# Attention and a SoLU feed-forward on one core: two spreads rescheduled, one PSUM bank exchanged, the last results stored in quarters

## The chip, the core and the metric

The kernel runs on one core of a Trainium2 chip. The metric is the device time of one execution in microseconds (us); a kernel's time is the median of its runs. Five engines run side by side, each in its own order: TensorE (PE, matrix products), VectorE (DVE), ScalarE (ACT), GpSimd (POOL) and SyncE (SP), which here issues nearly all transfers. TensorE writes into PSUM[...].

## The reference

```python
q_n, k_n = rmsnorm(q, g_q), rmsnorm(k, g_k)          # 8 x 12 heads, 448 x 64
scores = scale * np.matmul(q_n, k_n.transpose(0, 1, 3, 2))
attn = softmax(scores)
x = np.matmul(attn, v)           # bridged to 3584 tokens x 768
h = x @ w_in                     # 3584 x 1024
solu = h * softmax(h)
ln = (solu - mu) / np.sqrt(var + 1e-06) * g_ln
return ln @ w_out                # 3584 x 768
```

The names `softmax` and `rmsnorm` stand for the reference's own lines, which subtract the row's maximum and divide by the root of the mean square. All arithmetic is float32 in the kernel.

## The kernel before

`fast_path` does the work in three stages that follow each other on TensorE.

**Stage one**, to about 331 us, is attention. It leaves x in DRAM (`xd`).

**Stage two**, 331.7 to about 584 us, is `x @ w_in` and the SoLU with its normalisation. The 3584 tokens are 28 tiles t of 128 rows, two to a group g, so 14 groups; tiles 24 and 25 are group 12, tiles 26 and 27 group 13. A group is multiplied as a 2 x 2 block product with seven products instead of eight (`products`, p1 to p7, six matmuls of 512 columns each). They accumulate in four banks called A, B, C and D. `mul` (L974) takes banks A and C from the tag "t" (three tiles of two banks each, of which one bank is used) and B and D from the tag "o" (two tiles of one bank). B is used by two products: p5 starts it, `plus` (L998, VectorE) reads it, and p3, the last product of a group, writes on into the same bank. `plus` keeps a running row maximum, and p4 and p3 end with `done(1)` and `done(0)`, which complete the rows of tiles 2g+1 and 2g.

Each finished tile then goes through steps on other engines: `ff_max` (VectorE, at once), `ff_exp` (ScalarE, L1053), `ff_mult` (VectorE, L1057), `ff_moments` (VectorE L1065 to L1070, then two small GpSimd instructions, L1071 a power and L1073 the shift), `ff_norm` (ScalarE, L1077) and `ff_spread` (L1084). A spread is one VectorE transpose of 128 x 1024 (L1086) into a buffer `ub`, and four stores of 128 KB from it to DRAM (`ud`, L1089) on SP.

**Stage three**, from about 585 us, is the product with `w_out`. Four tiles make one n, so seven of them; for each n, `load_u` (L1128) brings eight pieces of 256 KB back from `ud`, `make` (L1144) turns them into operands called a11, a12, a22, s1 to s4 (a11, a12 and a22 are ScalarE copies, L1149, L1151 and L1153; the others VectorE), and `outer_product` (L1177) runs seven block products P1 to P7 of seven small products each (four matmuls of 192 columns). Its banks are A to C under tags of their own, placed over the eight banks that stage two gives back; in the kernel before, the first A of stage three is the bank that B of group 13 held. `plus` of this stage (L1202) moves a bank out: as a ScalarE copy (L1206; the temporaries q1, u2 and u3) for the first products, else as a VectorE sum (L1208). p7's result u3 must be out of bank A before p4 of the same product may write on into it. Finished quarters of an output block are summed on VectorE (L1226, L1238, L1246, L1208), and `store_y` (L1258) stores a block of 256 x 384 in one transfer of 384 KB. Of the seven products P2, P3 and P4 end a block; a fourth block, C22, is summed by `both` (L1264).

**The order of the work** is written out by hand. `unit(f)` emits one piece and moves a counter `now` by four; in stage three each slot moves it by one. `later(u, f)` puts f behind the piece that ends u units later. The pieces emitted this way are each engine's order, and no engine overtakes within it. `done` schedules the five steps of a tile by the list WAITS (L1117): 1, 2, 3, 5 and 7 units later. With seven units the spread of tile 25 comes after the last but one product of stage two, those of tiles 24, 27 and 26 fall into stage three, after its slots 3, 19 and 23. SP's order at the seam is: the four stores of tile 25; six loads for n = 0 (tiles 2 and 3 in two halves, then the second halves of tiles 0 and 1, which are a12); the four stores of tile 24; six loads for n = 1; the stores of tile 27; two loads; the stores of tile 26. The two a12 copies are placed at slots 10 and 11.

Of the kernel before, what the change touches and what calls it, by code (L numbers as in the profile page):

```python
# [366 lines left out]
def fast_path(  # L367
# [24 lines left out]
    nc = tc.nc  # L392
    B, H, S, D = q.shape
    DM, DFF = moe_w_in.shape
    P = 128
# [6 lines left out]
    HO = DM // 2  # L402
    NT = B * S // P
    NG = NT // 2
# [563 lines left out]
    def products(g, done):  # L968


        k = {}
        n = DFF // 2

        def mul(bank, a, i, begin=True):  # L974
            a11, a12, a21, a22 = gs[g, "A"]
            sm = gs[g, "s"]
            a = {"a11": a11, "a12": a12, "s3": a21, "a22": a22, "s1": sm[:, 0], "s2": sm[:, 1], "s4": sm[:, 2]}[a]
            if begin:
                tag = "t" if bank in "AC" else "o"
                k[bank] = ps_t.tile([P, 512], FP32, tag=tag, name=bank, bufs=3 if tag == "t" else 2)[:, 0:n]  # L980
            for c in range(HD):
                nc.tensor.matmul(  # L982
                    k[bank], a[:, c], w_in[i][:, c],
                    start=begin and c == 0, stop=c == HD - 1, skip_group_check=not begin,
                )

        def part(name, bank):
            k[name] = sums_in.tile([P, 512], FP32, tag="part", name=name, bufs=4)[:, 0:n]
            nc.scalar.copy(k[name], k[bank])

        def plus(row, col, bank, x):
            t = 2 * g + row
            d = mt.setdefault(t, {})
            out = half_of(t, col)
            top = small.tile([P, 1], FP32, tag="top", name="top")
            nc.vector.tensor_tensor_reduce(  # L998
                out, k[bank], k[x], 1.0, d.get("top", -3.4e38), OP.add, OP.max, top
            )  # L1000
            d["top"] = top

        def p1():
            mul("A", "a11", 0)
            part("q1", "A")

        def p2():
            mul("C", "a12", 1)
            plus(0, 0, "C", "q1")

        def p6():
            mul("A", "s2", 5, False)
            part("u2", "A")

        def p5():
            mul("B", "s1", 3)

        def p7():
            mul("A", "s3", 4, False)
            part("u3", "A")  # L1020
            plus(1, 1, "B", "u3")

        def p4():
            mul("D", "a22", 6)
            plus(1, 0, "D", "u3")
            done(1)

        def p3():
            mul("B", "s4", 2, False)
            plus(0, 1, "B", "u2")  # L1030
            done(0)

        return {1: p1, 2: p2, 3: p3, 4: p4, 5: p5, 6: p6, 7: p7}

    def half_of(t, i):
        d = mt.setdefault(t, {})
        if "h" not in d:
            d["h"] = big.tile([P, DFF], FP32, tag="h", name="h", bufs=3)
        return d["h"][:, i * DFF // 2 : (i + 1) * DFF // 2]
# [4 lines left out]
    def ff_max(t):  # L1044
        d = mt[t]
        d["nmax"] = small.tile([P, 1], FP32, tag="hmax", name="hmax")
        nc.vector.tensor_scalar(d["nmax"], d["top"], -1.0, None, OP.mult)  # L1047
# [46 lines left out]
    def in_parts():  # L1094
        def done(g, i):
            t = 2 * g + i
            ff_max(t)
            for x, f in zip(WAITS, (ff_exp, ff_mult, ff_moments, ff_norm, ff_spread)):
                later(x, lambda f=f: f(t))

        p = [products(g, lambda i, g=g: done(g, i)) for g in range(NG)]
        parts = [p[0][1], p[0][2]]
        for g in range(NG):
            turn = [p[g][6], p[g][5], p[g][7], p[g][4], p[g][3]]
            x = len(parts)
            if g + 1 < NG:
                turn[3:] = [p[g + 1][1], p[g][4], p[g + 1][2], p[g][3]]
            parts += turn
            if g + 1 < NG:
                follow(parts, x, lambda g=g: sizes(g + 1))  # L1110
                follow(parts, x + 1, lambda g=g: block_sums(g + 1, 0))
                follow(parts, x + 2, lambda g=g: block_sums(g + 1, 1))
            if g + 2 < NG:
                follow(parts, x + 4, lambda g=g: load_x(g + 2))
        return parts

    WAITS = (1, 2, 3, 5, 7)  # L1117
    ORDER = ("P1", "P5", "P6", "P2", "P7", "P3", "P4")
    STEP = 7
    PLACES = (0, 4, 8, 10, 12, 16, 20)  # L1120
    NS = NT // 4
    KC = HF // 2
    N2 = HO // 2
    HALVES = {"P1": ("a11", 0), "P2": ("a12", 1), "P6": ("s2", 5), "P5": ("s1", 3), "P7": ("s3", 4), "P3": ("s4", 2), "P4": ("a22", 6)}
    last = {}
    us = {}
# [50 lines left out]
    def outer_product(n, name, q):  # L1177


        operand_name, area = HALVES[name]  # L1180
        k = {}

        def mul(bank, a, i, begin):
            x = us[n, operand_name]
            sm = us.get((n, operand_name, "sums"))
            a = {
                "a11": x[:, 0, 0:KC], "a12": x[:, 0, KC:], "a22": x[:, 1, KC:],
                "s1": sm and sm[:, 0], "s2": sm and sm[:, 1], "s3": sm and sm[:, 2], "s4": sm and sm[:, 3],
            }[a]
            if begin:  # L1190
                tag = f"{bank}{q % 2}" + (str(q // 2 % 2) if bank == "A" else "")
                k[bank] = last["ps"].tile([P, 512], FP32, tag=tag, name=bank)[:, 0:N2]
            for c in range(KC):
                nc.tensor.matmul(  # L1194
                    k[bank], a[:, c].rearrange("p a i -> p (a i)"), w_out[:, area, i, c],
                    start=begin and c == 0, stop=c == KC - 1, skip_group_check=not begin,
                )

        def quarter(x, t, i):
            return x[:, t, i * N2 : (i + 1) * N2]  # L1200

        def plus(out, bank, t, i):  # L1202

            x = {"P6": "Q1", "P2": "Q1", "P7": "U2", "P4": "U3", "P3": "V"}.get(name)
            if x is None:
                nc.scalar.copy(out, k[bank])  # L1206
            else:
                nc.vector.tensor_tensor(out, k[bank], quarter(us[n, x], t, i), OP.add)  # L1208

        def temp(x):  # L1210
            k[x] = last["u"].tile([P, N2], FP32, tag=x, name=x, bufs=3)
            return k[x]

        def result(t, i):
            return quarter(us[n, name], t, i)

        def p1():
            mul("A", "a11", 0, True)
            plus(temp("q1"), "A", 0, 0)

        def p2():
            mul("C", "a12", 1, True)
            us[n, name] = out_tile(name)
            if name in ("P1", "P6", "P7"):
                us[n, {"P1": "Q1", "P6": "U2", "P7": "U3"}[name]] = us[n, name]
            nc.vector.tensor_tensor(result(0, 0), k["C"], k["q1"], OP.add)  # L1226

        def p6():
            mul("A", "s2", 5, False)
            plus(temp("u2"), "A", 0, 1)  # L1230

        def p5():
            mul("B", "s1", 3, True)

        def p7():
            mul("A", "s3", 4, False)
            plus(temp("u3"), "A", 1, 1)
            nc.vector.tensor_tensor(result(1, 1), k["B"], k["u3"], OP.add)  # L1238

        def p4():  # L1240
            mul("A", "a22", 6, False)
            plus(result(1, 0), "A", 1, 0)

        def p3():
            mul("B", "s4", 2, False)
            nc.vector.tensor_tensor(result(0, 1), k["B"], k["u2"], OP.add)  # L1246
            if name in ("P2", "P3", "P4"):
                store_y(n, us[n, name], *{"P2": (0, 0), "P3": (0, 1), "P4": (1, 0)}[name])

        return [p1, p2, p6, p5, p7, p4, p3]  # L1250

    def out_tile(name):
        tag = "huhuhubb"[len(turns) % 8]
        turns.append(tag)
        x = big.tile([P, DFF], FP32, tag=tag, name=name, bufs=2 if tag == "b" else 3)
        return x[:, 0 : 2 * HO].rearrange("p (t n) -> p t n", t=2)

    def store_y(n, x, k, i):  # L1258
        r = (4 * n + 2 * k) * P
        nc.sync.dma_start(  # L1260
            out[r : r + 2 * P, i * HO : (i + 1) * HO].rearrange("(t p) n -> p t n", p=P), x
        )

    def both(n, x, t):  # L1264

        if (n, x) not in us:
            us[n, x] = out_tile(x)
        nc.vector.tensor_tensor(us[n, x][:, t], us[n, "U2" if x == "V" else "U3"][:, t], us[n, "P5"][:, t], OP.add)
        if x == "C22" and t == 0:
            store_y(n, us[n, x], 1, 1)  # L1270

    def follow(p, i, f):
        g = p[i]

        def both():
            g()
            later(1, f)

        p[i] = both
# [7 lines left out]
    def later(units, f):  # L1287
        todo.append((now + 4 * units, f))
# [49 lines left out]
    with tc.manual_schedule():  # L1338
# [233 lines left out]
        for n in range(NS):  # L1572
            base = period * n
            for i, name in enumerate(ORDER):
# [4 lines left out]
                x = HALVES[name][0]  # L1579
# [118 lines left out]
```

## Time and profile before

| | |
|---|---|
| median of three runs | 825.22 us |
| the runs | 825.22, 827.1, 821.57 us |
| the profiled execution | 824.41 us, of which its span 822.2 |
| TensorE's clock in it | 0.997 of full speed |
| stage two on TensorE | 331.7 to 584.4 us of the span |
| stage three on TensorE | 585.2 to 816.0 us of the span |
| last store of a result | issued at 816.43 us, landed 3.9 us later |

Times within a profile are microseconds from the start of its span. A row of the timeline is: start, duration, engine, source line, operation, output tile <- input tiles, shapes, how many instructions are merged; in brackets how long the engine stood idle before, and what released it. A row of the waits is: engine, tile and line that waited <- what ended the wait: microseconds in total, times, longest. The engine name SPq is SP's queue of transfers. "Landing" is the time from the issue of a transfer to its completion.

### The profile page before, as it was taken

Reading aid. Unit: us, or ns where it says so; the run is one execution under the profiler, and the core shown is the slowest. Engines: PE = TensorE matmul, PEld = TensorE weight load, DVE = VectorE, ACT = ScalarE, POOL = GpSimd, SP = SyncE. Lnnn points to the kernel's source line nnn. Section 1 sums busy time; section 2 is a strip of 40 time slices with the busy share of each in tenths; the row PEclk is TensorE's granted clock in tenths of the full one; section 3 lists DMA queues with packets and bytes.
Section 4 is the critical chain, followed back from the end, with each engine's and each line's share of the span. In section 5 each row is a group of like instructions: output and inputs, shape, how many; then the busy total and the mean of one; then the engine's idle time right before and its main releaser. Section 6 shows DMA issues by size and latency. Waiting matters only on the chain.

```text
span 822.2 us, 14988 instructions
## 1 busy us (share of the span) xinstructions
PE 800.5 (97%) x5030; PEld 468.7 (57%) x5030; DVE 618.1 (75%) x1217; ACT 474.6 (58%) x785; POOL 468.7 (57%) x635
## 2 busy tenths in 40 slices
PE   8989999999999999999999999999799999999996
PEld 4333444433334443444444444444499999999996
DVE  6867888887788888377878766677886866866945
ACT  6667778776777767366667644444424464464420
POOL 1334545555555647333356467777387777877861
PEclk9999999999999999999999999999999999999999
DMA  7678777777777663335665335552448466376312
GB/s 132 142 134 200 145 183 177 176 153 171 154 176 180 126 156 117 89 102 125 189 169 150 91 98 133 136 140 70 140 142 269 130 207 231 128 241 200 128 59 82
DMA packets 271938, 122.74 MB, mean 149 GB/s; under 512 B 190444, under 2 KB 257004, under 8 KB 271852
## 3 DMA queue, kind: packets, MB, share of 16 engines
q1 hardware_dynamic: 256668, 111.79, 52.9%
q10 hardware_dynamic: 15184, 9.90, 4.5%
q8 instruction: 42, 0.69, 0.4%
q14 instruction: 44, 0.36, 0.1%
HBM read 84.94 MB, written 36.70 MB: 148 GB/s over the span
## 4 chain that ended last, share of the span: by engine, by line
PE 84%; SPq 2%; DVE 2%; issue 2%; POOL 1%; DMA 1%; ACT 1%; POOLq 0%; ACTq 0%; DVEq 0%
PE A L1194 15%; PE A L982 13%; PE o L865 10%; PE s L812 10%; PE B L982 8%; PE B L1194 8%; PE D L982 4%; PE C L982 4%; PE sm L884 4%; PE C L1194 4%; SPq L634 2%; PE s L825 2%; PE o L854 2%; POOL ss L674 1%; DMA ur<-ud 1%
## 5 line engine op out<-in xcount | busy, mean ns | idle before, releaser
L802 ACT ACTIVATE E<-s 128x896 f32<-128x896 f32 x168 | 139.0, 935 | 14.9 <-PE s L812 14.6
L812 PE MATMUL s<-qkT 64*64 64x448 f32 x1152 | 121.3, 548 | 1.5 <-ACT E L802 0.9
L865 PE MATMUL o<-E,v 128*64 128x448 f32 x576 | 113.5, 543 | 0.0
L674 POOL COPY ss<-part 32x56 f32<-32x56 f32 x88 | 42.1, 478 | 97.9 <-DVE part L664 95.2
L713 POOL TENSOR_TENSOR qkn<-qk,ny 128x896 f32<-128x896 f32 x46 | 77.1, 1697 | 28.2 <-DMA qk<-in_k_dram 12.0
L1071 POOL TENSOR_TENSOR he<-he,mhalf 128x1 f32<-128x1 f32 x28 | 28.1, 1005 | 106.7 <-DVE he L1070 106.2
L812 PEld LDWEIGHTS s<-qkT 64*64 64x64 f32 x1152 | 47.5, 163 | 61.1 <-ACT E L802 31.3
L865 PEld LDWEIGHTS o<-E,v 128*64 128x64 f32 x576 | 39.2, 137 | 72.7 <-issue 66.4
L1194 PE MATMUL B<-w_out,sums 128*128 128x192 f32 x392 | 80.5, 328 | 0.0
L1194 PE MATMUL A<-w_out,sums 128*128 128x192 f32 x392 | 80.0, 327 | 0.4 <-DVE u L1208 0.4
L982 PE MATMUL B<-w_in,xsum 128*128 128x512 f32 x168 | 76.7, 592 | 0.0
L982 PE MATMUL A<-w_in,xg 128*128 128x512 f32 x168 | 74.7, 593 | 0.0
L1053 ACT ACTIVATE u<-h,hmax 128x1024 f32<-128x1024 f32 x28 | 32.2, 1148 | 65.2 <-DVE hmax L1047 65.2
L1194 PEld LDWEIGHTS B<-w_out,sums 128*128 128x128 f32 x392 | 67.0, 191 | 0.1
L1194 PEld LDWEIGHTS A<-w_out,sums 128*128 128x128 f32 x392 | 66.2, 190 | 0.9 <-POOL sums L1175 0.6
L664 DVE TENSOR_REDUCE part<-sq 128x28 f32<-128x896 f32 x46 | 48.7, 1080 | 8.8 <-ACT sq L656 6.7
L982 PEld LDWEIGHTS B<-w_in,xsum 128*128 128x128 f32 x168 | 31.9, 190 | 40.2 <-issue 38.3
L982 PEld LDWEIGHTS A<-w_in,xg 128*128 128x128 f32 x168 | 31.8, 190 | 40.2 <-issue 39.1
L723 DVE STREAM_TRANSPOSE qkT<-qkn 128x896 f32<-128x896 f32 x46 | 48.9, 1093 | 6.6 <-POOL qkn L713 6.6
L839 DVE TENSOR_TENSOR es<-E 128x896 f32<-128x896 f32 x48 | 53.3, 1112 | 0.5 <-ACT E L802 0.5
L656 ACT ACTIVATE sq<-qk 128x896 f32<-128x896 f32 x46 | 43.6, 985 | 8.7 <-DMA qk<-in_k_dram 6.7
L1194 PE MATMUL A<-w_out,s 128*128 128x192 f32 x224 | 45.6, 326 | 0.0
(151 smaller groups left out, 1625.3 us busy)
## 6 DMA issues: line engine op xcount, KB each, us to landing
ur<-ud SPq DMA_DIRECT2D x60, 256.0 KB, 4.7
ud<-ub SPq DMA_DIRECT2D x112, 128.0 KB, 2.3
xd<-xo SPq DMA_DIRECT2D x24, 448.0 KB, 3.7
qk<-in_q_dram SPq DMA_DIRECT2D x184, 56.0 KB, 2.5
qk<-in_k_dram SPq DMA_DIRECT2D x184, 56.0 KB, 2.4
v<-in_v_dram SPq DMA_DIRECT2D x24, 384.0 KB, 4.4
out_dram<-P SPq DMA_DIRECT2D x21, 384.0 KB, 3.8
raw<-in_moe_w_in_dram SPq DMA_DIRECT2D x12, 512.0 KB, 5.2
```

The source lines that it names most:

```text
L656: nc.scalar.activation(d["sq"], d["qk"].rearrange("p s b d -> p (s b) d"), AF.Square)
L664: nc.vector.tensor_reduce(norms[m]["part"][:, i], st[n]["sq"], AX, OP.add)
L674: e.tensor_copy(ss[g * 32 : g * 32 + 32], part[o * 32 : o * 32 + 32])
L713: e.tensor_tensor(d["qkn"], d["qk"].rearrange("p s b d -> p (s b) d"), y.rearrange("p b -> p b ()").to_broadcast([P, 2 * NB, 32]), OP.mult,)
L723: nc.vector.transpose(d["qkT"].rearrange("p s t -> p (s t)"), d["qkn"].rearrange("p b d -> p (b d)"))
L802: nc.scalar.activation(d["E", kc], s[:, :, 0:S], AF.Exp)
L812: nc.tensor.matmul(s[c : c + D, h, 0:S], d["qkT"][hh, 1, keys], d["qkT"][hh, 0, :], start=True, stop=True,)
L839: nc.vector.tensor_tensor(d["es"], d["E", 0], d["E", 1], OP.add)
L865: nc.tensor.matmul(d["o"][h * D : (h + 1) * D, :], quads[n // 2]["v"][:, n % 2 * 2 + h, kc], d["E", kc][:, h], start=False, stop=(kc == NJ ...
L884: nc.tensor.matmul(sm[g : g + 32, :], ones[:, w], e[:, h, t * S // 2 : (t + 1) * S // 2], start=(x == 0), stop=(x == len(terms) - 1),)
L982: nc.tensor.matmul(k[bank], a[:, c], w_in[i][:, c], start=begin and c == 0, stop=c == HD - 1, skip_group_check=not begin,)
L1194: nc.tensor.matmul(k[bank], a[:, c].rearrange("p a i -> p (a i)"), w_out[:, area, i, c], start=begin and c == 0, stop=c == KC - 1, skip_gr ...
```

## The change

Four things are altered; no arithmetic changes.

- Tile 25's spread comes 5 units after its rows are complete instead of 7, tile 26's 8 instead of 7. All others keep 7. In VectorE's order the transpose of tile 25 moves from behind `ff_max` of tile 27 to directly behind `ff_mult` of tile 24, ahead of the moments of tile 24 and of the sums from banks B and D of group 13. The transpose of tile 26 moves back past four sums of stage three. In SP's order no transfer passes another.
- B of group 13 is allocated under the tag "t". By the allocation this is the bank that stage three first uses for the B of its second product; stage three's first A then falls on D of group 13.
- For the last n, the blocks of P3 and P4 are stored by quarters, each as soon as it is summed: eight transfers of 96 KB in place of two of 384 KB. A row of a transfer is then 768 bytes instead of 1536.
- The remaining stores are as before.

```diff
-                tag = "t" if bank in "AC" else "o"
+                tag = "t" if bank in "AC" or bank == "B" and g == NG - 1 else "o"
...
-            for x, f in zip(WAITS, (ff_exp, ff_mult, ff_moments, ff_norm, ff_spread)):
+            spread = {NG - 2: 7 - 2 * i, NG - 1: 8 - i}.get(g, 7)
+            for x, f in zip((1, 2, 3, 5, spread), (ff_exp, ff_mult, ff_moments, ff_norm, ff_spread)):
                 later(x, lambda f=f: f(t))
...
-    WAITS = (1, 2, 3, 5, 7)
...
+        block = {"P2": (0, 0), "P3": (0, 1), "P4": (1, 0)}.get(name)
+        by_quarter = n == NS - 1 and name in ("P3", "P4")
+
+        def stored(t, i):
+            if by_quarter:
+                store_quarter(n, us[n, name], *block, t, i)
...
             nc.vector.tensor_tensor(result(0, 0), k["C"], k["q1"], OP.add)
+            stored(0, 0)
...
             nc.vector.tensor_tensor(result(1, 1), k["B"], k["u3"], OP.add)
+            stored(1, 1)
...
             plus(result(1, 0), "A", 1, 0)
+            stored(1, 0)
...
             nc.vector.tensor_tensor(result(0, 1), k["B"], k["u2"], OP.add)
-            if name in ("P2", "P3", "P4"):
-                store_y(n, us[n, name], *{"P2": (0, 0), "P3": (0, 1), "P4": (1, 0)}[name])
+            stored(0, 1)
+            if block and not by_quarter:
+                store_y(n, us[n, name], *block)
...
+    def store_quarter(n, x, k, i, t, half):
+        r = (4 * n + 2 * k + t) * P
+        c = i * HO + half * N2
+        nc.sync.dma_start(out[r : r + P, c : c + N2], x[:, t, half * N2 : (half + 1) * N2])
```

## The prediction

> **What bounds the kernel now.** I read the page's totals, then TensorE's waits, then the two places where it stands still, engine by engine in order of time.
>
> ```profile
> PE 800.5 (97%) x5030; PEld 468.7 (57%) x5030; DVE 618.1 (75%) x1217; ACT 474.6 (58%) x785; POOL 468.7 (57%) x635
> PE A L1194 <- ACT u L1206: 4.5, 1, 4.5
> PE sm L884 <- DVE es L839: 3.2, 5, 1.2
> ...
> PE A L1194 <- DVE top L998: 0.9, 1, 0.9
> ```
>
> TensorE (PE) is busy 97% of the span: the change can win only waits, slow-clock time and the tail after the last matmul. Both waits of A L1194 shown lie where stage two gives way to stage three. TensorE, and below it the windows (us; PE, PEld, DVE, ACT and POOL busy; granted clock; DMA share; GB/s):
>
> ```profile
> 581.64 2.74 PE L982 MATMUL B<-w_in,xsum 128*128 128x512 f32 x6
> 585.23 0.92 PE L1194 MATMUL A<-w_out,a 128*128 128x192 f32 x4 [0.85 <-DVE top L998]
> ...
> 590.53 0.81 PE L1194 MATMUL A<-w_out,sums 128*128 128x192 f32 x4
> 595.87 1.65 PE L1194 MATMUL A<-w_out,a 128*128 128x192 f32 x4 [4.53 <-ACT u L1206]
> ...
> 594.00:595.00 1.00, 0.00 (x0) 0.00 (x0) 0.84 (x5) 1.00 (x1) 0.09 (x1) 1.00 0.84 261
> ...
> 597.00:598.00 1.00, 1.00 (x5) 1.00 (x5) 0.37 (x1) 1.00 (x2) 1.00 (x2) 0.50 1.02 393
> ```
>
> After the 4.53 us hole the granted clock is 0.50: groups of four matmuls start 1.45, 1.28 and 0.92 us apart instead of 0.65, 1.7 us lost. Why the hole lasts until 595.87 is read from ScalarE (ACT), GpSimd (POOL) and VectorE (DVE):
>
> ```profile
> 588.13 0.32 ACT L1206 COPY u<-A 128x192 f32<-128x192 f32 x1 [0.33 <-PE A L1194]
> 593.34 0.62 ACT L1151 COPY a<-ur 128x512 f32<-128x512 f32 x1 [4.89 <-DMA ur<-ud]
> 593.86 1.24 ACT L1077 ACTIVATE u<-u,shift,he 128x1024 f32<-128x1024 f32 x1
> 595.01 0.60 ACT L1151 COPY a<-ur 128x512 f32<-128x512 f32 x1
> 595.51 0.30 ACT L1206 COPY u<-A 128x192 f32<-128x192 f32 x1
> ...
> 592.70 0.27 POOL L1073 TENSOR_SCALAR shift<-mv,he 128x1 f32<-128x1 f32 x1
> ...
> 576.50 1.29 DVE L1065 BATCH_NORM_STATS2 bs<-u 128x6 f32<-128x512 f32 x2
> ...
> 582.81 1.25 DVE L1086 STREAM_TRANSPOSE ub<-u 128x1024 f32<-128x1024 f32 x1
> ...
> 585.28 1.22 DVE L1057 TENSOR_TENSOR u<-h,u 128x1024 f32<-128x1024 f32 x1
> ```
>
> ScalarE works in order. The copy u3 that frees TensorE (595.51) stands behind two copies of operand a12 (L1151) and, between them, the norm of tile 27 (L1077). The first a12 copy waits for the fifth load of stage three, which stands in SP's queue behind the four stores of tile 25's spread, which wait for the transpose at 582.81. That norm was itself ready only at 592.97 (592.70 + 0.27), just 0.89 us before it ran: two chains end almost together, and the profile names one.
>
> **What the Trainium skill says.** "TensorE: Matmul & The Clock Gate", What's actually happening: after an idle window of about 3.4 us the clock halves, after as much activity it recovers, and the window runs free. The trace agrees: half clock after 4.53 us, full again near 599. "PSUM — Partial Sum Buffer", PSUM bank collisions: guard a bank, not an address; here TensorE waits 0.85 us for VectorE to finish reading the bank that stage three takes first. "DMA: Bandwidth & Descriptors", Anatomy of one DMA: a fixed part near 2 us, mostly the write receipt, plus bytes, fitted on the software path. The 128 KB ud stores here land in 2.3 us (median), the last 384 KB output store in 3.9. The same section puts semaphore waits on the issuing sequencer, as on SP here.
>
> **Part 1, tile 25's spread two units earlier.** One transpose and its four SP DMAs (about 0.45 us of issue each) move; nothing is added. SP has nothing else between, and the six loads follow the stores as before. The transpose now stands before the moments of tile 24, and needs the norm of tile 25, which ran 577.27 to 578.51. So VectorE, free at 576.47, parks 2.1 us, transposes 578.54 to 579.78 (1.24), and SP issues from there, not from 584.07: 4.29 us earlier. With the same 9.27 us from transpose to landing (584.07 to 593.34) the first a12 copy can run at 589.05.
> Behind the parked transpose:
> - The moments of tile 24 go from 576.50 to 579.70, +3.2. Their chain is ready 2.06 later at 581.76; an idle POOL needs 1.39 for the power and 0.27 for the shift (before, warm, 0.55). Norm 24 runs at 583.70 instead of 581.00, to 584.94.
> - The first sum from bank B (L998) goes from 579.93 to 581.76, done 582.45. Stage two's last product writes on into that bank at 581.64 and so waits **0.8 us, new**. It ends 585.2.
> - exp of tile 27 stands behind norm 24: 584.84 instead of 582.88, to 586.1. Its multiply on VectorE goes from 585.28 to 586.13, **+0.85**. The last sum from B leads to the same 586.1 by the late product.
> - VectorE has no gap from there to tile 27's moments (before: 585.28 to 590.98), so norm 27 is ready at 592.97 + 0.85 = 593.82. Second a12 copy 594.97, u3 595.47, TensorE **595.83 against 595.87**.
>
> The load was 4.3 us too late and is early now; the norm takes its place as what is late. Gain 0.04. The hole is a little shorter (exp 26 ends 587.5, so q1 and the next product come 0.5 late and the matmuls before it end at 591.8): 4.0 us, still over the 3.4 of the page, and I leave the clock loss in. Lower bound: the clock stays full, -1.7. Without VectorE's delay, TensorE could start at 594.98, -0.9.
>
> **Part 2, the other bank.** By allocation order B of the last group moves from the bank that stage three's first product takes to one it uses much later (bank 6, first written for the second product's B). The 0.85 us wait goes. But part 1 made the last product end 0.8 late, so stage three begins at 585.2 as before; and any start before the hole is swallowed by it, since its end hangs on ScalarE. Bounds 0 and -0.85; taken 0.
>
> **Part 3, tile 26's spread one product later.** Transpose and four stores move from 603.88 past four small VectorE instructions to about 605. TensorE's starts there slip 0.12 in all (603.42, 604.11, 604.84 instead of every 0.65); taken -0.1. Nothing on SP is passed, and its data are read only for the last n, over 140 us later (loads from 750 on).
>
> **Part 4, quarters.** Two 384 KB stores of the last n (P3, P4) become eight of 96 KB: six more SP issues of 0.37 us. SP is empty there (before: stores at 807.27, 813.58, 815.08, 816.43) and each quarter comes at least 0.3 us after the one before; the last is still issued at 816.43, after the last VectorE result. It then carries a quarter, with nearly nothing queued. Landing 3.9 becomes between 2.3 (128 KB ud stores) and 2.7 (96 KB raw loads): -1.2 to -1.6. The poorest gain is bytes alone, 288 KB at the 362 GB/s of the stretch from 816 to 817, -0.8; nothing if the short rows of 768 B cost what the bytes save. Taken -1.3.
>
> **Sum.** 0.0 + 0.0 - 0.1 - 1.3 = -1.4 us. The profiled execution takes 824.41 (span 822.2 and 2.2 around it), so 823.0; it lies 0.8 under the median of 825.22, where the sum gives **823.8**.
>
> **Rivals.**
> - *The load alone held the hole* (0.12). The chain named in the profile runs through it. Then a12 at 589.05 lets u3 follow its product: -4.53, -1.7 of clock, -1.4: 817.6. Against it: norm 27, 0.89 us behind.
> - *The clock stays full* (0.22): the shorter hole misses a whole window. 823.8 - 1.7 = 822.1.
> - *Parked VectorE, slower* (0.13): if the 3.2 us by which tile 24's moments slip reach tile 27's multiply whole instead of 0.85, norm 27 is ready at 596.2, TensorE starts 2.3 late, less 0.8 of tail: 826.7. Above a delay of 2.2 us (0.89 of slack plus 1.3 of tail) the change loses. VectorE's 2.7 us of gaps between 578.7 and 584.4 speak against it.
> - *The quarters change nothing* (0.05): the write receipt rules the tail. 825.1.
>
> **How the numbers follow.** My case has 0.48. The three runs of before spread from 821.57 to 827.1, so a median of a few runs can sit 2 us off. With that on both sides of 822 to 824, 820.3 to 826.8 leaves out most of the first rival and the outer half of the slow one. One per cent (8.25 us) is what a measurement can tell from no change; even the best rival reaches -7.6, so faster by it gets 0.03, slower 0.03, within 0.94.
>
> **What would show it.** Right: a VectorE transpose standing from 576.5 to 578.5; a TensorE wait near 0.8 before stage two's last product and none at stage three's first; a hole still ending near 595.8, with the second a12 copy behind norm 27; last landing near 2.5 us. Wrong: a12 copies still waiting for DMA, norm 27 ready before 593, or a hole under 3 us.

## The result and the profile after

| | before | after |
|---|---|---|
| median of 12 runs each | 825.24 us | 826.64 us |
| range of the runs | 821.57 to 827.4 | 821.29 to 828.86 |
| the profiled execution (span) | 824.41 (822.2) | 827.41 (825.1) |
| stage two, start to the product into bank D of group 13 | 247.39 | 248.21 |
| from that product to the end of the last matmul | 236.95 | 238.17 |
| from there to the end of the span | 6.14 | 6.09 |

The ratio is 1.0013, 95% interval 0.9992 to 1.0033: no difference that can be measured. The median is 2.8 us above the predicted 823.8 and just inside the range, which went to 826.8. Between the two profiled spans lie 3.0 us, and 1.82 of them arise before the change reaches TensorE: stage two starts 1.0 us later and takes 0.82 more to the last product into D, with the same instructions on TensorE. So both profiles, and those of the experiments, are compared from the start of that product (579.06 before, 580.88 after), written +t.

TensorE of the changed kernel, from its timeline:

```profile
584.18 2.81 PE L982 MATMUL B<-w_in,xsum 128*128 128x512 f32 x6 [0.56 <-POOL he L1071]
586.83 0.81 PE L1194 MATMUL A<-w_out,a 128*128 128x192 f32 x4
...
589.66 0.89 PE L1194 MATMUL A<-w_out,sums 128*128 128x192 f32 x4 [0.72 <-ACT q L1206]
...
597.63 1.65 PE L1194 MATMUL A<-w_out,a 128*128 128x192 f32 x4 [3.83 <-ACT u L1206]
599.07 1.49 PE L1194 MATMUL B<-w_out,sums 128*128 128x192 f32 x4
600.35 1.49 PE L1194 MATMUL C<-w_out,s 128*128 128x192 f32 x4
601.63 1.45 PE L1194 MATMUL A<-w_out,sums 128*128 128x192 f32 x4
602.91 0.82 PE L1194 MATMUL B<-w_out,sums 128*128 128x192 f32 x4
```

Stage two's last product now waits: it starts 3.30 us after the one before it, against 2.58. The wait at stage three's first product is gone, and it starts at +5.95 instead of +6.17. The hole ends at +16.75 instead of +16.81. The bracket names GpSimd's `he`, which merely signalled last (done at 584.05). By the program this product waits for VectorE's late sum from bank B, done at 584.02. Then VectorE and ScalarE:

```profile
580.24 1.25 DVE L1086 STREAM_TRANSPOSE ub<-u 128x1024 f32<-128x1024 f32 x1 [2.08 <-ACT u L1077]
581.41 1.24 DVE L1065 BATCH_NORM_STATS2 bs<-u 128x6 f32<-128x512 f32 x2
...
583.34 0.68 DVE L998 CUSTOM_DVE_ANT_0 h<-B,u 128x512 f32<-128x512 f32 x1
...
587.89 1.22 DVE L1057 TENSOR_TENSOR u<-h,u 128x1024 f32<-128x1024 f32 x1
```

```profile
590.80 0.62 ACT L1151 COPY a<-ur 128x512 f32<-128x512 f32 x1
595.61 1.24 ACT L1077 ACTIVATE u<-u,shift,he 128x1024 f32<-128x1024 f32 x1 [4.19 <-POOL shift L1073]
596.76 0.60 ACT L1151 COPY a<-ur 128x512 f32<-128x512 f32 x1
597.27 0.31 ACT L1206 COPY u<-A 128x192 f32<-128x192 f32 x1
```

VectorE stands 2.08 us at the transpose of tile 25, and the sum from bank B comes after it. The first a12 copy waits for no load any more. ScalarE then stands 4.19 us ahead of the norm of tile 27, with the second a12 copy and u3 behind it. The work that held TensorE was exchanged for another piece on the same engine, at the same time.

The clock after the hole, in windows of the kernel before and then of the changed one (columns as in the prediction; the granted clock is the third number from the right):

```profile
595.00:600.00 5.00, 4.13 (x15) 4.13 (x16) 2.43 (x6) 3.94 (x9) 4.82 (x7) 0.66 0.68 225
600.00:605.00 5.00, 5.00 (x33) 4.86 (x32) 4.36 (x8) 1.16 (x3) 4.84 (x8) 1.00 0.48 132
```

```profile
595.00:600.00 5.00, 2.37 (x7) 2.37 (x8) 4.20 (x12) 4.39 (x8) 2.81 (x5) 0.61 0.59 190
600.00:605.00 5.00, 5.00 (x23) 5.00 (x23) 1.89 (x4) 1.58 (x5) 4.89 (x8) 0.71 0.37 123
```

Before, full clock was back by 600; after, the half clock lasts into the next window. Over the six groups of matmuls that follow the hole it costs 2.69 us, against 1.70 (their starts, less 0.65 us each).

At the end of the program, SP's own waits after its last store, before and then after:

```profile
SPq L1666 <- SPq L1666: 3.3, 1, 3.3
...
SPq L1693 <- PEq L1693: 0.6, 2, 0.5
```

```profile
SPq L1682 <- SPq L1682: 2.6, 1, 2.6
SPq L1709 <- SPq L1709: 1.1, 1, 1.1
...
SPq L1709 <- PEq L1709: 0.2, 1, 0.2
```

The last store lands 3.1 us after its issue instead of 3.9. SP's first wait is 0.7 us shorter, and the program's close, the lines below it, takes that back: 1.3 us of waits against 0.6. None of these is a wait for the landing. Before, SP came to its wait for the last store at 820.77, 0.40 us after that store had landed; in the changed kernel 0.38 us after. In the changed kernel's wait of 1.1 us VectorE and ScalarE stand still too, for 0.96 us.

### The profile page after: what moved, and what is told of

It is laid out like the page before. It is cut to its first block, busy times and chain, and to the rows that moved or that the text cites. A ratio compares the mean times of both kernels' runs of the same rounds, so it can differ in the third digit from the quotient of the medians.

```text
span 825.1 us, 14999 instructions
## 1 busy us (share of the span) xinstructions
PE 802.1 (97%) x5030; PEld 469.7 (57%) x5030; DVE 617.7 (75%) x1217; ACT 474.6 (58%) x785; POOL 468.5 (57%) x635
## 4 chain that ended last, share of the span: by engine, by line
PE 72%; SPq 6%; DVE 5%; DMA 4%; POOL 2%; issue 2%; ACT 2%; DVEq 0%; ACTq 0%; POOLq 0%
PE A L1194 15%; PE A L982 11%; PE B L1194 8%; PE o L865 7%; PE s L812 7%; PE B L982 7%; SPq L634 5%; PE C L982 4%; PE D L982 4%; PE C L1194 4%; PE sm L884 3%; DMA v<-in_v_dram 1%; PE s L825 1%; PE o L854 1%; DMA qk<-in_k_dram 1%
```

## The experiments

All ratios are to the kernel before, run on the same chip. "Seam" is the time from group 13's product into D to the last matmul's end in the profile: 236.95 before, 238.17 changed. Line numbers in some kernels are one higher. Each seam is that of one profile. Two kernels, "quarters alone" and "quarters of P4 alone", have the seam's instructions of the kernel before, and theirs are 237.56 and 236.47: a difference of that size between two seams shows nothing by itself.

| kernel | median, us | ratio (95%) | seam, us |
|---|---|---|---|
| changed, norm 27 later | 823.9 | 0.9999 (0.9976 to 1.0022) | 236.35 |
| before, norm 27 later | 824.28 | 0.9987 (0.9964 to 1.001) | 237.16 |
| spread of tile 25 alone | 825.08 | 1.0008 (0.9992 to 1.0023) | 237.79 |
| bank alone | 825.68 | 0.9995 (0.9972 to 1.0019) | 238.53 |
| quarters alone | 824.49 | 0.9995 (0.9978 to 1.0012) | 237.56 |
| quarters of P4 alone | 824.88 | 0.9988 (0.997 to 1.0005) | 236.47 |
| load and norm both behind | 824.61 | 0.9981 (0.9966 to 0.9997) | 236.44 |
| VectorE's rest later | 823.49 | 0.998 (0.9962 to 0.9997) | 236.05 |
| last tiles' moments later | 822.93 | 0.9963 (0.9948 to 0.9978) | 234.56 |
| last tiles' steps all later | 822.54 | 0.9956 (0.9939 to 0.9972) | 233.99 |
| the same, set apart | 820.8 | 0.9953 (0.9937 to 0.9969) | 233.49 |
| steps later, old start of the seam | 822.71 | 0.9981 (0.9962 to 1.0) | 235.43 |

**Is it norm 27 that holds the hole?** In both kernels it is put behind u3.

```diff
+            norm = 6 if g == NG - 1 and i == 1 else 5
-            ... (1, 2, 3, 5, spread) ...
+            ... (1, 2, 3, norm, spread) ...
```

In the changed kernel:

> The changed kernel, and the norm of tile 27 one unit later, so that ScalarE does it after the copy u3 instead of ahead of it. Nothing else moves. Theory (the early load has made the norm of tile 27 what comes last): the copies of a12 and u3 follow each other near 11 us after the start of group 13's D product, the 3.83 us hole before P1's fourth product goes (under 0.5), and the next thing late is VectorE's sum of bank B with u3, which P1's last product needs: a wait of about 2.3 us there. P1's last product starts 17.7 us after the start of the D product (22.0 in the changed kernel), the clock stays full, the whole is 2.5 to 4.4 us shorter than the changed kernel. Rival (the loads still hold ScalarE, the norm is not on the path): hole and hole's end as in the changed kernel, 16.75 us after the D product's start.

In the kernel before:

> The kernel before with the same move of the norm of tile 27 alone. Theory (two chains end together; in the kernel before the load is last by 0.9): the a12 copies still wait for the load, so only the norm's 1.15 us comes out: the hole ends about 15.8 us after the start of the D product instead of 16.8 and is still near 3.5 us; total 0 to 2.7 us shorter, the larger value if the clock stays full. Rival (the norm alone held the hole, and the load was never last): the hole is gone here too, as in the changed kernel with this move.

TensorE of the first:

```profile
588.02 0.81 PE L1195 MATMUL A<-w_out,a 128*128 128x192 f32 x4
...
592.95 0.92 PE L1195 MATMUL B<-w_out,sums 128*128 128x192 f32 x4 [2.17 <-DVE P L1247]
593.70 1.24 PE L1195 MATMUL A<-w_out,a 128*128 128x192 f32 x4
595.21 1.65 PE L1195 MATMUL A<-w_out,sums 128*128 128x192 f32 x4 [0.27 <-POOL sums L1174]
```

The hole is gone: P4's first product starts at +12.69 with no bracket. Four groups on, at +17.62, TensorE waits 2.17 us for a VectorE sum, and the clock halves even after this short hole. In the kernel before, the same edit leaves a hole of 3.64 us that ends at +15.92: there the load holds it. So load and norm each hold the hole when the other is out of the way. The changed kernel's seam gets 1.8 us shorter, less than the theory hoped for, which had the clock stay full; that of the kernel before doesn't, as 0.9 us of hole are gone and the half clock costs 1.2 more (2.87 against 1.70). Neither kernel's time differs measurably from the kernel before.

**The change's parts, one by one.** The spread of tile 25 at 5 units in the kernel before; the kernel before with the other bank; the changed kernel with the old bank and all spreads at 7.

```diff
+            spread = 5 if g == NG - 2 and i == 1 else 7
```

> The kernel before with the early spread of tile 25 alone (old bank, one store for a block, tile 26 as before). Theory: VectorE stands 2.1 us for the norm of tile 25, the last product of stage two waits 0.6 to 0.8, stage three's first product waits another 0.85 for its bank, and the hole still ends 16.8 us after the D product's start, the norm of tile 27 being last; so neither the earlier load nor the waits ahead of the hole change the time: within 0.1% of before. Rival (the load held it): the hole ends with the early load, near 12 us. Rival (each wait adds to the end): the hole ends 0.8 to 1.6 us later than before.

```diff
-                tag = "t" if bank in "AC" else "o"
+                tag = "t" if bank in "AC" or bank == "B" and g == NG - 1 else "o"
```

> The kernel before with the other bank alone. Theory (a wait ahead of a longer wait is worth nothing): no wait for VectorE at stage three's first product, which starts near +5.3 instead of +6.17 from the product into D; the hole at P4's first product ends at +16.8 as before and is 0.8 longer, 5.2 to 5.4 us; D to the last matmul 237 us, time as before. Rival (the start of stage three carries the hole along): hole end near +16.0, 0.8 us won.

```diff
-            spread = {NG - 2: 7 - 2 * i, NG - 1: 8 - i}.get(g, 7)
+            spread = 7
```

> The kernel before with the stores by quarters alone. Theory (the last store's bytes and what queues ahead of it count): SP's wait after the last issue falls from 3.3 us to 2.3 to 2.7 us, and the stretch from the end of the last matmul to the end of the span from 6.2 to 5.2 to 5.6 us. Rival (the receipt of the last write rules, whatever its size): 3.3 and 6.2 as before, no change of the time. The hole ends as in the kernel before.

TensorE with the spread alone, and with the bank alone:

```profile
584.51 2.81 PE L982 MATMUL B<-w_in,xsum 128*128 128x512 f32 x6 [0.40 <-POOL he L1071]
588.18 0.92 PE L1195 MATMUL A<-w_out,a 128*128 128x192 f32 x4 [0.85 <-DVE top L998]
...
597.96 1.65 PE L1195 MATMUL A<-w_out,a 128*128 128x192 f32 x4 [3.67 <-ACT u L1207]
```

```profile
583.87 0.81 PE L1194 MATMUL A<-w_out,a 128*128 128x192 f32 x4
...
595.85 1.65 PE L1194 MATMUL A<-w_out,a 128*128 128x192 f32 x4 [5.01 <-ACT u L1206]
```

With the spread alone both waits ahead of the hole are there, and the hole ends at +16.58, practically where it was. With the bank alone stage three starts 1.0 us earlier, at +5.15, the hole grows to 5.01 us and ends at +17.13, later rather than earlier. Neither gains anything. The bank's seam of 238.53 is no cost of the bank: 3.10 us of half clock, against 1.70, make most of its difference to before.

With the quarters alone the hole should have ended as before. It ended at +16.10, and at +15.95 with quarters of P4 alone (below), against +16.81, though nothing is altered there. ScalarE of the latter:

```profile
589.71 0.62 ACT L1151 COPY a<-ur 128x512 f32<-128x512 f32 x1 [3.67 <-DMA ur<-ud]
590.59 1.24 ACT L1077 ACTIVATE u<-u,shift,he 128x1024 f32<-128x1024 f32 x1 [0.26 <-POOL shift L1073]
```

Here the load is in by +13.04, and ScalarE waits for the norm's shift, which is ready at +13.9 as in the kernel before. Issued at the same place, the load landed at +14.25 in the kernel before, +14.58 with the bank alone, which is why that hole ended later, +13.54 with the quarters alone and +13.04 here. So which of the two holds the hole in the kernel before differs from one execution to the next.

**The end of the program.** The kernel before, with quarters for P4 only:

```diff
-        by_quarter = n == NS - 1 and name in ("P3", "P4")
+        by_quarter = n == NS - 1 and name == "P4"
```

> The kernel before with quarters for P4 of the last n alone: SP has three more stores instead of six. The last landing is 2.8 to 3.0 us by every theory, as with all quarters, against 3.7 to 3.9 with whole stores. If the 0.9 to 1.1 us that SP loses in the program's close with all quarters hang on how many instructions SP has, this loss is gone and from the last matmul to the end of the span it takes 5.3 us. If they belong to the earlier landing itself, it is 5.9 to 6.6 as in the runs with all quarters. Time against before: same in both cases.

| stores of the last n | kernels | last matmul to the end of the span, us |
|---|---|---|
| whole | before, norm 27 later in it, spread alone, bank alone | 6.14, 6.16, 6.23, 6.16 |
| P3 and P4 by quarters | changed, norm 27 later in it, quarters alone, both behind | 6.09, 5.88, 6.54, 6.13 |
| P4 by quarters | P4 alone, VectorE's rest later, and the four last | 5.90, 5.90, 5.88 to 5.91 |

With all quarters alone SP's first wait fell to 2.6 us, as its theory said, but the end took 6.54 us, above even the rival's 6.2. For P4 only, the expectation was wrong on the landing: the four quarters land after 3.7 us (median); P3's 384 KB are issued between them, which probably is the reason. On the close it was half right: the second wait of SP isn't there, but 5.9 is all it comes to. SP's waits with P4 alone by quarters:

```profile
SPq L1682 <- SPq L1682: 3.3, 3, 2.7
...
SPq L1709 <- PEq L1709: 0.6, 2, 0.5
```

The longest of the three at L1682, 2.7 us, is the jump over the general path; only the other two, 0.6 us together, wait for landings. In every kernel with quarters the jump is 2.6 to 2.7, however early the stores land. In the four with whole stores it is 3.3 to 3.4, and that is the 3.3 us wait shown for the kernel before. "Runtime: NRT & Kernel Launch" in the Trainium skill, Instruction fetch mechanics, says that a branch taken to code that isn't loaded stalls until it is fetched. The trace agrees: SP's branch is issued at once and its next instruction, a wait for a store that had landed before the branch, comes 2.6 us later in the changed kernel and 3.3 in the kernel before. No run here has a tail without this jump. Why it is shorter with quarters, and what the second wait with all quarters is, wasn't settled; a fetch of instructions runs during the latter, but that is no proof.

**What comes after load and norm?** Both are put behind u3 without parking VectorE.

```diff
-            spread = {NG - 2: 7 - 2 * i, NG - 1: 8 - i}.get(g, 7)
+            spread = {NG - 2: 7 - i, NG - 1: 8 - i}.get(g, 7)
+            norm = 6 if g == NG - 1 and i == 1 else 5
...
-        made(0, "a12", 10, 11)
-        made(0, "a22", 12, 14)
+        made(0, "a12", 12, 13)
+        made(0, "a22", 14, 15)
```

> The changed kernel with three places altered: tile 25's spread 6 units behind its rows instead of 5, tile 27's norm at 6 instead of 5, and the copies of a12 and a22 at slots 12 to 15. Neither the load nor the norm then stands ahead of u3, and VectorE isn't parked at tile 25's transpose. Times count from the start of stage two's product into bank D. Theory (the hole is the later of two things that stand ahead of u3 on ScalarE, and behind it waits VectorE's own work): no wait before stage two's last product, stage three starts near +5.3 instead of +5.95, no hole at P4's first product, in its place a wait for VectorE at P3's, whose product starts near +16.8 (+17.6 with the norm alone moved); from D to the last matmul 235.5 us or less, against 237.0 before and 238.2 changed. Rival (any gap halves the clock and VectorE's work comes due later anyway): P3's product again near +17.6, D to the end 236.4 or more, and a time equal to the kernel before within 0.2%.

Then VectorE's work that isn't due is put off as well, and from here on only P4 is stored by quarters:

```diff
-            norm = 6 if g == NG - 1 and i == 1 else 5
+            moments, norm = {2 * NG - 1: (3, 6), 2 * NG - 2: (5, 6)}.get(t, (3, 5))
...
-        made(0, "s3", 6, 8)
+        made(0, "s3", 13, 15)
```

> As the kernel with both moved, and further: VectorE's work that isn't due at the seam is put off (the moments of tile 26 to 5 units, its norm to 6, operand s3 to slots 13 and 15), and only P4 of the last n is stored by quarters. Theory (after the hole VectorE is what is late at the seam): the wait for VectorE at P3's product is under 1 us, the clock stays full or is halved for under 4 us, D to the last matmul 233 to 235 us, and the time 2 to 4 us (0.2 to 0.5%) under the kernel before. Rival (what is put off comes back as waits between 600 and 622, where VectorE is busy nearly all the time): waits for VectorE or GpSimd of 2 us and more in that stretch, D to the end 236 or more.

TensorE of the first of these, and VectorE of the second ahead of the sum that its TensorE waited for:

```profile
592.00 0.81 PE L1195 MATMUL A<-w_out,a 128*128 128x192 f32 x4
...
596.93 1.57 PE L1195 MATMUL B<-w_out,sums 128*128 128x192 f32 x4 [2.17 <-DVE P L1247]
```

```profile
596.95 1.28 DVE L1065 BATCH_NORM_STATS2 bs<-u 128x6 f32<-128x512 f32 x2
...
599.62 1.21 DVE L1162 TENSOR_TENSOR s<-a,s 128x512 f32<-128x512 f32 x1
...
601.29 1.23 DVE L1086 STREAM_TRANSPOSE ub<-u 128x1024 f32<-128x1024 f32 x1
602.45 0.31 DVE L1257 TENSOR_TENSOR P<-B,u 128x192 f32<-128x192 f32 x1
```

In the first, the start comes at +5.15, the hole at P4's product is gone and a wait for VectorE stands in its place, at +16.89, as the theory said; the half clock behind it and a seam of 236.44 are what the rival said. In the second this wait is gone too, and one of 2.21 us stands four groups later, with a seam of 236.05, again the rival's: the sum at 602.45 has the moments of tile 26, halves of s3 and s4 and the transpose of tile 27 ahead of it. VectorE has no idle time from 588.7 to 604 there. The wait is what VectorE is behind by; each edit only moves the place where TensorE meets it.

**Can the backlog be put off far enough?** Tiles 26 and 27 are read only for the last n, over 140 us later. What bounds their steps is that stage three's results take over their buffers: tile 27 must be spread before slot 25, tile 26 before slot 32.

```diff
-            moments, norm = {2 * NG - 1: (3, 6), 2 * NG - 2: (5, 6)}.get(t, (3, 5))
-            ... (1, 2, moments, norm, spread) ...
+            steps = {2 * NG - 1: (1, 2, 5, 7, 8), 2 * NG - 2: (1, 5, 7, 8, 9)}.get(t, (1, 2, 3, 5, 7 - (t == 2 * NG - 3)))
...
-        made(0, "a22", 14, 15)
-        made(0, "s4", 17, 20)
+        made(0, "a22", 17, 19)
+        made(0, "s4", 22, 25)
```

and s1 and s2 of the second n six slots later.

> The kernel with VectorE's rest later, and further: of the last two tiles, which are read only for the last n, everything that can wait waits (tile 27: moments 5, norm 7, spread 8 units behind its rows; tile 26: multiply 5, moments 7, norm 8, spread 9), s4 of the first n goes to slots 22 and 25, a22 to 17 and 19, and s1 and s2 of the second n six slots later. Theory (after the two waits ahead of u3, what holds TensorE at the seam is VectorE's backlog, and it can be put off into stage three): no wait over 1 us from stage three's first product to slot 20 (the product that started at +20.3 with VectorE's rest later starts near +18), clock full throughout, D to the last matmul 231 to 234 us against 236.05 there and 236.95 before, and a time 3 to 5 us (0.4 to 0.6%) under the kernel before. Rival (VectorE and GpSimd have no spare time in the first 40 us of stage three, so the backlog only moves): a wait for VectorE or GpSimd of 2 us or more between 600 and 625 with the clock halved after it, D to the end 235.5 or more, time within 0.25% of the kernel before.

The second kernel keeps tile 26's multiply at 2 units, s4 at 17 and 20, and the second n as it was:

> As the kernel with all of the last tiles' steps later, but tile 26's multiply at 2 units, s4 at slots 17 and 20, and the second n's operands where they were. Theory: the 2.1 us of tile 26's moments are gone from ahead of the sum that TensorE waited for (2.21 us with VectorE's rest later), so that wait falls under 0.5 us; D to the last matmul 232 to 235 us. Rival (the backlog only moves): a wait of 2 us or more up to 10 us later; D to the end 235.5 or more.

The third sets the long pieces apart, with steps of (1, 2, 5, 7, 7.5) and (1, 4, 7.25, 8.25, 9), s4 at 19 and 26, s1 and s2 of the second n at 36, 39, 44 and 46:

> The kernel with all of the last tiles' steps later, with VectorE's long pieces set apart from each other: tile 27's spread 7.5 units behind its rows, tile 26's multiply 4, moments 7.25, norm 8.25, spread 9; s4 of the first n at slots 19 and 26, s1 of the second n at 36 and 39, s2 at 44 and 46. Theory (the 1.77 us wait for VectorE at +23.35 there comes of a transpose and a set of moments that stand directly behind each other, 3.2 us, and the later waits of some 1.1 us of the second n's operands): that wait falls under 1 us, D to the last matmul 232 to 233.5 us against 233.99, time 0.1% better. Rival (the sum of VectorE's work up to 620 decides): 233.8 or more, no better.

TensorE's waits from 575 to 640 us in this third kernel, and its clock:

```profile
PE B L1194 <- DVE P L1256: 1.2, 2, 0.9
PE A L1194 <- ACT q L1206: 0.7, 1, 0.7
PE A L1194 <- DVE u L1208: 0.4, 1, 0.4
PE A L1194 <- POOL sums L1172: 0.2, 1, 0.2
```

```profile
585.00:590.00 5.00, 5.00 (x33) 5.00 (x32) 4.68 (x12) 2.73 (x7) 3.86 (x6) 1.00 0.73 190
590.00:595.00 5.00, 4.71 (x28) 4.15 (x27) 5.00 (x10) 2.94 (x6) 4.84 (x7) 1.00 0.83 268
595.00:600.00 5.00, 4.65 (x28) 4.24 (x27) 4.79 (x15) 1.24 (x1) 4.11 (x8) 1.00 0.70 189
```

The 3.8 us hole has become waits of under 1 us each, the clock stays at 1.00, and VectorE (third busy column) is as full as before. The theory holds in all three: the product that had waited 2.21 us starts at +17.40, with no wait, in the first kernel (0.60 us are left in the second, a little over what was expected); the largest wait left there is 1.77 us; in the third that product doesn't wait, and the next one does for 0.35. The time of the first and the third is 0.44% and 0.47% under the kernel before, 3.6 and 3.9 us; that the third is better than the first can't be told from these two. About 0.25 us of it is P4's quarters, by the tails above, and the rest lies in the seam.

**Were the change's first two parts worth nothing?** The kernel with all steps later, but with tile 25's spread at 7 and the old bank:

```diff
-            ... .get(t, (1, 2, 3, 5, 7 - (t == 2 * NG - 3)))
+            ... .get(t, (1, 2, 3, 5, 7))
...
-                tag = "t" if bank in "AC" or bank == "B" and g == NG - 1 else "o"
+                tag = "t" if bank in "AC" else "o"
```

> The kernel with all of the last tiles' steps later, but with tile 25's spread at 7 units and the bank as in the kernel before. Theory (waits ahead of a longer wait are worth nothing until that one is gone; here it is gone): the 0.85 us wait at stage three's first product is back and now counts, and the first copy of a12 waits for its load until near +14.3, so that TensorE waits for GpSimd's sums of a12 or another work behind it; D to the last matmul 1 to 3 us more than 233.99, time 0.1 to 0.4% more than there but still under the kernel before. Rival (the change's first two parts do nothing here either): 233.99 within 0.5 us.

Its TensorE waits, and ScalarE ahead of the first of them:

```profile
PE A L1194 <- ACT u L1206: 1.6, 1, 1.6
PE A L1194 <- DVE u L1208: 1.4, 1, 1.4
...
PE A L1194 <- DVE top L998: 0.9, 1, 0.9
```

```profile
595.38 1.33 ACT L1151 COPY a<-ur 128x512 f32<-128x512 f32 x2 [2.81 <-DMA ur<-ud]
596.61 0.31 ACT L1206 COPY u<-A 128x192 f32<-128x192 f32 x1
```

The bank's 0.85 us and the late load are both back, the load now ahead of a u3 copy that is due, and the seam is 1.44 us longer than that of the kernel with all steps later, as the theory said. So by the seam, in one profile each, the two parts count once the other waits are out of the way; before that they didn't. In the time it isn't shown: the intervals of the two ratios overlap.

## Why the prediction was right, and where not

- **Part 1** held in its mechanism, step by step: VectorE parked 2.08 us (predicted 2.1), tile 24's moments 3.09 later (3.2), the last product 0.72 late (0.8), tile 27's multiply 0.79 later (0.85). Only the small power of tile 24 was cheaper than assumed, 0.55 us instead of 1.39. That norm 27 takes the load's place is shown by moving it. That the hole's end came out 0.06 earlier, against 0.04 predicted, is in part luck: in two other profiles with the same instructions up to the hole's end as in the kernel before, where the load landed earlier, it ended 0.71 and 0.86 us earlier without any change.
- **Part 2** held: the wait went and nothing came of it, in the change or alone.
- **Part 3**, -0.1: no such gain. From the half clock's end on, 0.3 us of small slips came in the changed profile; no run isolates the move.
- **The clock** was left unchanged. It cost 0.99 more. Seven profiles have a hole of 3.6 to 5.0 us at this same product. By their records of the granted clock it stayed at half for 3.41 us in two of them, the kernel before and P4's quarters alone, and for 6.83 us in five. In the two it fell 0.14 us before TensorE resumed, and 0.78 us after; in the five 0.6 to 1.6 us before. TensorE lost about half of what was left of that time when it resumed: 1.70 and 1.78 us, against 2.65 to 3.15. With the same instructions up to there, the clock fell at +15.49, +16.67 and +16.73 (quarters alone, before, P4's quarters alone). So it wasn't the edit that set this term but where the hole met the fall of the clock, which is chance. "TensorE: Matmul & The Clock Gate", What's actually happening, has the window run free; the traces agree, as in all fourteen profiles every change of the clock comes a whole number of 3.413 us after the first entry of its record.
- **Part 4** is the term that was mis-sized: -1.3 predicted, -0.05 in the profile. The step that failed is to count "Landing 3.9 becomes between 2.3 and 2.7" as the end's gain. The last quarter landed after 3.1. And the end didn't wait for the landing, in the kernel before either: SP came to that wait 0.40 us after the store was in. What comes last is SP's jump, 3.3 us before and 2.6 after, and the close, which took the 0.7 back. The rival "the quarters change nothing" named the right size and another reason, the write receipt; the runs show the jump and the close instead.
- **The sum** was -1.4; the interval of the ratio, -0.7 to +2.7 us, excludes it. The median lies in the range that was given, at its edge, because the range left room for runs 2 us off on either side. In the profile the change itself makes -0.06 (hole) + 0.99 (clock) + 0.30 (slips) - 0.05 (end) = +1.2 us, and the stages ahead of it 1.82 more.
- Of the rivals, the load alone and the full clock are refuted by the changed profile itself (and in other kernels holes of about 2.2 us, shorter than the rival needed, halved the clock too), and the parked VectorE stopped at 0.79 of the 2.2 us that it needed.

## What to carry over

Before making what ends a wait come earlier, read what stands second on the same in-order engine and when that was ready: here 0.89 us separated them in one profile and in another the order was reversed, and the 0.79 us by which the edit delayed VectorE used up what the earlier load could give. Compare a second profile of the same kernel before a step of under a microsecond is counted: here the load's landing alone moved by 1.2 us between profiles of the same instructions. Removing a wait upstream of a longer one pays only after the longer one is gone, so a part that measures as nothing alone may be tried again then; here one pair of profiles supports it. If one wait after another appears behind each one removed, add up the work of the engine that they lead to: here VectorE was behind, and only work put off past the crowded stretch shortened the kernel by more than 0.2%.

## What was not expected of the hardware

- Holes of 2.17 us (twice) and 2.21 us were followed by half clock, which began 1.00, 0.11 and 0.90 us after TensorE had resumed; holes of 1.61 and 1.77 us were not. "TensorE: Matmul & The Clock Gate" gives an idle window of about 3.4 us; by these runs less than that is enough.
- In all these ten profiles the half clock lasted one window of 3.41 us or two. It lasted two in the five in which TensorE was idle for 0.6 us or more after the clock had fallen, and one in the others, where that was 0.14 us or nothing.
- After its last store SP needs 2.6 to 2.7 us, with whole stores 3.3 to 3.4, to reach the first instruction behind the jump. With whole stores as with eight quarters it came to its wait for the last store only after that store had landed. With eight quarters the close stood still once for 0.9 to 1.1 us; what that is stays open.
